# Loading k of the first 512 tokens four tokens to a partition, in a fused attention and feed-forward kernel

## The chip, the cores and the metric

The kernel runs on one core of one Trainium2 chip. The metric is the device time of one execution in microseconds (us). Engines: PE multiplies matrices, DVE (VectorE), ACT (ScalarE) and POOL (GpSimd) work on tiles, SP issues the transfers.

## The reference

Linear attention with a decay per head, on 4 batches x 8 heads x 768 tokens x 64, then a feed-forward layer (FFN) without activation on 3072 rows of 512:

```
for each block of tokens:                       # lam: one decay per head
    intra = ((q k^T) * Dmask) v                 # Dmask[i,j] = lam^(i-j) for i >= j
    inter = (q * lam^(pos+1)) kv_state
    out   = intra + inter
    kv_state = lam^block * kv_state + (k * lam^(block-1-pos))^T v
x = out as 3072 x 512
y = ((x @ w_a) * (x @ w_b)) @ w_out             # 512 -> 1536 -> 512
```

The kernel works in 24 "units" of 128 tokens, six to a batch. The powers of lam are multiplied onto q and k, so that scores only need a triangular mask.

## The kernel before

FFN groups follow each other; attention of later units is placed between their matmuls by a fixed plan. Before the first FFN group the attention of units 0 to 3 must be done. Only that part changes. All loads go through one queue in program order: q, k, v of the first four units, then w_a and w_b in chunks of 512 KB.

```python
q4_r = q[0, :, 0:PACK * BLK, :].rearrange("h (p r) d -> p h (r d)", r=PACK)   # PACK = 4
for i in range(2):                       # q: four tokens to a partition, 1 KB runs, four heads each
    t = wst_pool.tile([128, 1024], F32, name="q4", tag="wst")
    nc.sync.dma_start(out=..., in_=q4_r[:, 4 * i:4 * i + 4])
for w in "kv":                           # k and v: unit by unit, one token to a partition
    for u in range(n0):                  # n0 = 4
        load_x(w, u)                     # [128 tokens, 8 heads, 64], runs of 256 bytes
pump()                                   # then the weights
# ... cut: q scaled and transposed in two halves of four heads ...
for u in range(n0):
    start_unit(u, "pool" if u else "dve")      # scale k: unit 0 on DVE, 1 to 3 on POOL
transpose_k(0); warm(6)                        # warm(n): n idle matmuls
for u in range(n0 - 1):
    transpose_k(u + 1)
    piece_S(u)                                 # scores on PE, two masks on DVE
    warm(4)
make_vb(0, "pool"); kv_update(0); kv_copy(0, "act")
kq3 = scores(3)
make_vb(1, "pool")
for u in range(n0):
    if 0 < u < n0 - 1:
        kv_update(u)                           # state matmuls, all in one PSUM bank
        kv_copy(u, "act" if u < 2 else "dve")  # state to SBUF
        make_vb(u + 1, "pool")
    inter(u)                                   # q with the state: needs the copy of unit u-1
    if u == n0 - 1:
        cast_w("a", 0, "dve")
    intra(u)                                   # masked scores with v
    warm(4)
    # ... cut: masks of unit 3 ...
    evac_o(u, xT, col)                         # o_ps to the FFN's input, on ACT
cast_w("b", 0, "dve")
```

Later units scale k on DVE or POOL and q on POOL, and cast v on POOL (units 4 to 6) or DVE (from 7). Banks of PSUM, the memory that PE writes, come from a ring of seven, of which the idle matmuls hold one until the FFN starts.

## Time and profile before

| | before |
|---|---|
| time, median of 3 (lowest to highest) | 237.23 us (237.14 to 237.46) |
| span in the profile | 235.5 us |
| busy: PE / DVE / ACT / POOL | 96% / 48% / 39% / 22% |
| first FFN matmul | 20.33 us |
| last output of units 0 to 3 | 19.40 us |

In a line of the timeline, the first number is the start in us from the span's start, the second the length, then engine, source line, operation, result and operands; the bracket at the end tells how long the engine was idle before and what ended it. In the chain of waits each step is what released the next.

### The profile page before, as it was taken

The page shows a single profiled execution, that of the slowest core. Times are in us where ns is not written, and L with a number is a line of the kernel's source. Part 1 is how long each engine was busy: PE and PEld are TensorE (multiplying, and loading weights), DVE is VectorE, ACT ScalarE, POOL GpSimd, SP SyncE. Part 2 cuts the span into 40 slices and gives each one's busy share as a digit, 9 for nine tenths or more (in the row PEclk, how much of TensorE's full clock was granted, in tenths as well). Part 3 has the DMA queues.
Part 4 walks back from the last instruction along what each step waited for, and adds up shares of the span by engine and source line. Part 5 has one row for each costly group of instructions (what it writes and reads, how often), then busy time and mean ns, then how long its engine had stood idle before and what let it go on. Part 6 is the DMA issues. An engine that isn't in the chain of part 4 may idle for free.

```text
span 235.5 us, 4537 instructions
## 1 busy us (share of the span) xinstructions
PE 226.3 (96%) x1767; PEld 125.6 (53%) x1767; DVE 113.2 (48%) x200; ACT 91.6 (39%) x172; POOL 51.1 (22%) x64
## 2 busy tenths in 40 slices
PE   7597999999999999999999999999999999999994
PEld 2464444458698754454544454544454544444494
DVE  0584756835558637665135575035565215332050
ACT  3463665046455542342143242142341242332151
POOL 6360000144344743303305503003300000000000
PEclk9999999999999999999999999999999999999999
DMA  4999999999999999999929959713120210000311
GB/s 153 234 245 351 348 357 346 281 214 274 238 236 211 216 171 235 253 190 150 224 91 215 186 60 219 170 62 85 36 47 0 89 71 23 0 0 0 121 60 49
DMA packets 97382, 38.32 MB, mean 163 GB/s; under 512 B 85328, under 2 KB 92880, under 8 KB 97360
## 3 DMA queue, kind: packets, MB, share of 16 engines
q1 hardware_dynamic: 97216, 38.02, 73.1%
q8 instruction: 14, 0.23, 0.5%
q14 instruction: 8, 0.07, 0.1%
q10 hardware_dynamic: 144, 0.00, 0.0%
HBM read 28.32 MB, written 6.29 MB: 147 GB/s over the span
## 4 chain that ended last, share of the span: by engine, by line
PE 88%; SPq 5%; DMA 3%; ACT 1%; DVE 1%; issue 1%; DVEq 0%
PE a_ps L401 27%; PE b_ps L401 27%; PE op L422 26%; SPq L125 5%; DMA wst<-in_moe_w_a_dram 3%; PE o_ps L338 2%; PE kq L314 2%; PE kvd L357 2%; PE o_ps L330 1%; PE tps L291 1%; ACT o_sb L417 1%; SPq L202 0%; DVE wa_sb L158 0%; DVE m L322 0%; ACT xT L345 0%
## 5 line engine op out<-in xcount | busy, mean ns | idle before, releaser
L413 DVE TENSOR_TENSOR ab<-a_sb,b_ps 128x512 bf16<-128x512 bf16 (+2 forms) x96 | 52.6, 552 | 80.9 <-PE b_ps L401 58.8
L401 PE MATMUL a_ps<-xT,wa_sb 128*128 128x512 bf16 (+2 forms) x384 | 77.1, 326 | 1.8 <-DVE wa_sb L158 1.2
L401 PE MATMUL b_ps<-xT,wb_sb 128*128 128x512 bf16 (+2 forms) x384 | 77.2, 326 | 0.0
L408 ACT CAST a_sb<-a_ps 128x512 bf16<-128x512 f32 (+2 forms) x96 | 45.6, 481 | 65.1 <-PE a_ps L401 64.2
L422 PE MATMUL op<-wo_sb,ab 128*128 128x512 bf16 (+2 forms) x312 | 65.6, 363 | 0.0
L401 PEld LDWEIGHTS <-wb_sb 128*128 128x128 bf16 x384 | 34.5, 98 | 28.6
L401 PEld LDWEIGHTS <-wa_sb 128*128 128x128 bf16 x384 | 33.6, 98 | 28.7 <-DVE wa_sb L158 1.4
L422 PEld LDWEIGHTS <-ab 128*128 128x128 bf16 x312 | 28.6, 98 | 30.2
L322 DVE TENSOR_TENSOR m<-kq,lotri 128x512 bf16<-128x512 f32 x48 | 29.9, 682 | 21.3 <-PE kq L314 21.2
L253 POOL TENSOR_TENSOR qk<-kf,lp_k 128x512 bf16<-128x512 f32 x20 | 21.5, 1073 | 81.7 <-issue 31.4
L417 ACT COPY o_sb<-op 128x512 f32<-128x512 f32 (+2 forms) x26 | 14.2, 554 | 37.2 <-PE op L422 37.2
L258 POOL TENSOR_TENSOR qk<-qf,lp_q 128x512 bf16<-128x512 f32 x20 | 22.2, 1111 | 26.3 <-DMA qf<-in_q_dram 26.3
L345 ACT CAST xT<-o_ps 128x512 bf16<-128x512 f32 x24 | 13.2, 589 | 17.4 <-PE o_ps L338 17.3
L370 DVE TENSOR_TENSOR st<-kvd,bdiag 128x512 bf16<-128x512 f32 x18 | 12.3, 684 | 4.4 <-PE kvd L357 4.4
L293 ACT COPY qkT<-tps 128x1024 bf16<-128x1024 bf16 x7 | 7.1, 1012 | 10.9 <-PE tps L291 10.9
L191 PE MATMUL idle<-idle_sb 128*128 128x128 bf16 (+1 forms) x55 | 8.6, 292 | 1.3 <-DVE idle_sb L186 1.3
L338 PE MATMUL o_ps<-m,vb 128*64 128x128 bf16 x192 | 8.2, 223 | 0.0
L267 DVE CAST vb<-vf 128x512 bf16<-128x512 f32 x17 | 7.9, 466 | 0.0
L357 PE MATMUL kvd<-vb,qk 128*128 128x128 bf16 x80 | 7.8, 219 | 0.0
L357 PEld LDWEIGHTS <-qk 128*128 128x128 bf16 x80 | 5.9, 98 | 3.4 <-ACT st L368 0.2
L330 PEld LDWEIGHTS <-st 128*128 128x128 bf16 x80 | 5.5, 98 | 2.8 <-DVE st L370 0.2
L314 PEld LDWEIGHTS <-qkT 64*128 64x128 bf16 x192 | 5.4, 94 | 2.4 <-issue 0.6
(42 smaller groups left out, 74.4 us busy)
## 6 DMA issues: line engine op xcount, KB each, us to landing
kf<-in_k_dram SPq DMA_DIRECT2D x24, 256.0 KB, 5.0
vf<-in_v_dram SPq DMA_DIRECT2D x24, 256.0 KB, 5.0
out_dram<-o_sb SPq DMA_DIRECT2D x23, 256.0 KB, 2.2
qf<-in_q_dram SPq DMA_DIRECT2D x20, 256.0 KB, 4.4
wst<-in_moe_w_a_dram SPq DMA_DIRECT2D x6, 512.0 KB, 8.6
wst<-in_moe_w_b_dram SPq DMA_DIRECT2D x6, 512.0 KB, 8.7
wst<-in_moe_w_out_dram SPq DMA_DIRECT2D x6, 512.0 KB, 8.5
q<-in_q_dram SPq DMA_DIRECT2D x2, 512.0 KB, 5.5
```

Of the source, the lines that this page charges most:

```text
L253: eng_of(eng).tensor_mul(qk[:, 1], raw.pop((u, "k")), lp_k[:, u % NB].to_broadcast([128, H, D]))
L258: eng_of(eng).tensor_mul(U[u]["qk"][:, 0], raw.pop((u, "q")), lp_q[:, u % NB].to_broadcast([128, H, D]))
L322: nc.vector.tensor_mul(m, kq[i], lotri_bc)
L338: nc.tensor.matmul(d["o"][p, hp, :], lhsT=d["vb"][:, 2 * hp + i, :], rhs=d["m"][i][:, hp, :], start=(u % NB == 0 and hp == 0), stop=True, ...
L345: nc.scalar.copy(xT[:, :, col:col + BLK], o_ps)
L357: nc.tensor.matmul(kv["ps"][:, hp, :, :], lhsT=d["qk"][:, 1, 2 * hp:2 * hp + 2, :], rhs=d["vb"][:, 2 * hp:2 * hp + 2, :], start=(nb == 0 a ...
L370: nc.vector.tensor_mul(st[:].rearrange("p hp i d -> p hp (i d)"), kv["ps"][:].rearrange("p hp i d -> p hp (i d)"), bdiag_bc)
L401: nc.tensor.matmul(ps[:, :gt], lhsT=w_sb[:, s, f * 128:(f + 1) * 128], rhs=xT[:, s, :gt], start=(s == 0), stop=(s == KS - 1))
L408: nc.scalar.copy(a_sb[:, :gt], ps[:, :gt])
L413: nc.vector.tensor_mul(ab[:, f, :gt], a_sb[:, :gt], ps[:, :gt])
L417: nc.scalar.copy(o_sb[:, lo:hi], op[:, lo:hi])
L422: nc.tensor.matmul(op[:, lo:hi], lhsT=ab[:, f, t * 128:(t + 1) * 128], rhs=wo_sb[:, f, lo:hi], start=(f == 0), stop=(f == FC - 1))
```

## The change

The intent: k of the first 512 tokens goes through the queue as fast as q, in 1 KB runs, so that w_a comes sooner. Its transposed form comes out as q's does. The natural form (tokens on partitions), which the state needs, is then made by transposing back. The states after units 0, 1 and 2 are summed in three banks at once, so that no state matmul waits for the copy before it.

```diff
-    for w in "kv":
-        for u in range(n0):
-            load_x(w, u)
+    for w, src in (("q", q), ("k", k)):
+        x4_r = src[0, :, 0:PACK * BLK, :].rearrange("h (p r) d -> p h (r d)", r=PACK)
+        for i in range(2):
+            ...
+    for u in range(n0):
+        load_x("v", u)
 # ... cut
+    def scale4(w, i):                    # half i: four heads
+        for eng, rs in ((nc.vector, slice(0, 3)), (nc.gpsimd, slice(3, 4))):
+            eng.tensor_mul(...)          # three quarters on DVE, one on POOL
+    def natural_k(i, eng):
+        tps = ps_bank("tn", [128, PACK, 2, 128], BF16)
+        # 8 transposes of kT back, one copy of 128x1024
 # ... cut
+    for i in range(2):
+        scale4("q", i); transpose4("q", i); warm(4)
+    for i in range(2):
+        scale4("k", i); transpose4("k", i); warm(4)
     for u in range(n0):
+        make_vb(u, "pool")
+    scores4(0)                           # four heads of all four units; 4 banks, then 4 masks
+    natural_k(0, "act")
+    warm(4)
+    scores4(1)
+    natural_k(1, "act")
+    sts = [ps_bank("kv0", ...), ps_bank("kv1", ...), kv_bank()]
+    for hh in range(2):
+        for u, ps in enumerate(sts):
+            for w in range(u + 1):
+                kv_mms(ps, w, range(2 * hh, 2 * hh + 2), w == 0)
+            if hh:
+                kv_copy(u, ps, ("act", "dve", "act")[u])
     for u in range(n0):
         inter(u)
         intra(u)
-        warm(4)
+        warm(2)
+        evac_o(u, *xTs[u], eng="dve" if u == 2 else "act")
+    cast_w("a", 0, "both")               # half on DVE, half on POOL
```

More of the change, by code (lines that the diff above doesn't have):

```diff
@@ L156, in cast_w @@
             nc.scalar.copy(dst, t)
+        elif eng == "both":
+            nc.vector.tensor_copy(dst[:, :, :128], t[:, :, :128])
+            nc.gpsimd.tensor_copy(dst[:, :, 128:], t[:, :, 128:])
         else:
@@ L196 @@
                                                 ap=[[0, 128], lam.ap[0]]))
-    q4 = []
-    q4_r = q[0, :, 0:PACK * BLK, :].rearrange("h (p r) d -> p h (r d)", r=PACK)
-    for i in range(2):
-        t = wst_pool.tile([128, 1024], F32, name="q4", tag="wst")
-        nc.sync.dma_start(out=t[:].rearrange("p (h x) -> p h x", h=4),
-                          in_=q4_r[:, 4 * i:4 * i + 4])
-        q4.append(t[:].rearrange("p (h r d) -> p h r d", h=4, r=PACK))
-        staged["q4", i] = t
-    for w in "kv":
-        for u in range(n0):
-            load_x(w, u)
+    x4 = {}
+    for w, src in (("q", q), ("k", k)):
+        x4_r = src[0, :, 0:PACK * BLK, :].rearrange("h (p r) d -> p h (r d)", r=PACK)
+        for i in range(2):
+            t = wst_pool.tile([128, 1024], F32, name=w + "4", tag="wst")
+            nc.sync.dma_start(out=t[:].rearrange("p (h x) -> p h x", h=4),
+                              in_=x4_r[:, 4 * i:4 * i + 4])
+            x4[w, i] = t[:].rearrange("p (h r d) -> p r h d", h=4, r=PACK)
+            staged[w + "4", i] = t
+    for u in range(n0):
+        load_x("v", u)
     pump()
@@ L235 @@
     lp_q = singles.tile([128, NT, H, 1], F32, name="lp_q")
-    lp_k = singles.tile([128, NB, H, 1], F32, name="lp_k")
+    lp_k = singles.tile([128, NT, H, 1], F32, name="lp_k")
     nc.vector.tensor_mul(tmpe, _bc(loglam, [loglam.ap[0], [0, NT], loglam.ap[1]]),
@@ L239 @@
     nc.scalar.activation(lp_q[:, :, :, 0], tmpe, AF.Exp)
-    nc.scalar.activation(lp_k[:, :, :, 0], tmpe[:, :NB], AF.Exp, scale=-1.0)
+    nc.scalar.activation(lp_k[:, :, :, 0], tmpe, AF.Exp, scale=-1.0)
     lotri_bc = _bc(lotri, [lotri.ap[0], [0, HP], lotri.ap[1]])
@@ L254, in make_ks @@
                                lp_k[:, u % NB].to_broadcast([128, H, D]))
-        U[u] = dict(qk=qk)
+        U[u] = dict(qk=qk, kn=qk[:, 1])
     def make_qs(u, eng):
@@ L294, in piece_T @@
         d["qT"], d["kT"] = qkT[:, 0], qkT[:, 1]
-    def transpose_k(u):
-        d = U[u]
-        tps = ps_bank("tpk", [128, HP, 128], BF16)
-        for hp in range(HP):
-            nc.tensor.transpose(tps[:, hp, :], d["qk"][:, 1, 2 * hp:2 * hp + 2, :], ident)
-        qkT = qkT_pool.tile([128, 2, HP, 128], BF16, name="qkT", tag="qkT")
-        nc.scalar.copy(qkT[:, 1], tps)
-        d["kT"] = qkT[:, 1]
     def score_banks():
@@ L318, in masks, with mask @@
     def masks(u, kq):
-        U[u]["m"] = []
+        ms = mask(kq)
+        U[u]["m"] = lambda i, hp: ms[i][:, hp, :]
+    def mask(kq):
+        ms = []
         for i in range(2):
@@ L322, in masks @@
             nc.vector.tensor_mul(m, kq[i], lotri_bc)
-            U[u]["m"].append(m)
+            ms.append(m)
+        return ms
     def inter(u):
@@ L338, in intra @@
                 nc.tensor.matmul(d["o"][p, hp, :], lhsT=d["vb"][:, 2 * hp + i, :],
-                                 rhs=d["m"][i][:, hp, :], start=(u % NB == 0 and hp == 0),
+                                 rhs=d["m"](i, hp), start=(u % NB == 0 and hp == 0),
                                  stop=True, skip_group_check=True)
@@ L347, in evac_o, with kv_mms, kv_bank, kv_copy @@
             nc.vector.tensor_copy(xT[:, :, col:col + BLK], o_ps)
-    def kv_update(u):
-        d = U[u]
-        nb = u % NB
-        if nb == NB - 1:
-            return
-        if nb == 0:
-            kv["ps"] = kvps_pool.tile([128, HP, 2, D], F32, name="kvd", tag="kvd")
-        for hp in range(HP):
-            nc.tensor.matmul(kv["ps"][:, hp, :, :], lhsT=d["qk"][:, 1, 2 * hp:2 * hp + 2, :],
-                             rhs=d["vb"][:, 2 * hp:2 * hp + 2, :],
-                             start=(nb == 0 and hp == 0), stop=True, skip_group_check=True)
-    def kv_copy(u, eng="dve"):
+    def kv_mms(ps, w, hps, first):
+        d = U[w]
+        for hp in hps:
+            nc.tensor.matmul(ps[:, hp, :, :], lhsT=d["kn"][:, 2 * hp:2 * hp + 2, :],
+                             rhs=d["vb"][:, 2 * hp:2 * hp + 2, :], start=(first and hp == 0),
+                             stop=True, skip_group_check=True)
+    def kv_bank():
+        kv["ps"] = kvps_pool.tile([128, HP, 2, D], F32, name="kvd", tag="kvd")
+        return kv["ps"]
+    def kv_update(u):
         if u % NB == NB - 1:
             return
+        if u % NB == 0:
+            kv_bank()
+        kv_mms(kv["ps"], u, range(HP), u % NB == 0)
+    def kv_copy(u, ps, eng="dve"):
         st = st_bufs[u % 4]
@@ L367, in kv_copy @@
                 p = slice(64 * i, 64 * i + 64)
-                nc.scalar.copy(st[p, :, i, :], kv["ps"][p, :, i, :])
+                nc.scalar.copy(st[p, :, i, :], ps[p, :, i, :])
         else:
             nc.vector.tensor_mul(st[:].rearrange("p hp i d -> p hp (i d)"),
-                                 kv["ps"][:].rearrange("p hp i d -> p hp (i d)"), bdiag_bc)
+                                 ps[:].rearrange("p hp i d -> p hp (i d)"), bdiag_bc)
     def piece_S(u):
@@ L377, in piece_V @@
         kv_update(u)
-        kv_copy(u)
+        if u % NB < NB - 1:
+            kv_copy(u, kv["ps"])
     xTs = {}
@@ L479, with transpose4 @@
     new_xT(0)
-    scratch = ab_pool.tile([128, FC, 512], BF16, name="scratch", tag="ab")
-    qs4 = scratch[:, 0:4, :].rearrange("p r (h d) -> p r h d", d=D)
-    qT4 = scratch[:, 4:8, :]
-    for i in range(2):
-        hs = slice(4 * i, 4 * i + 4)
-        nc.vector.tensor_mul(qs4[:, :, hs, :].rearrange("p r h d -> p h r d"), q4[i],
-                             lp_q[:, NB:, hs, :].rearrange("p r h o -> p h r o")
-                             .to_broadcast([128, 4, PACK, D]))
-        tps = ps_bank("tq", [128, 2, PACK, 128], BF16)
+    scr = [ab_pool.tile([128, FC, 512], BF16, name="scratch", tag="ab") for _ in range(2)]
+    xs4 = {"q": scr[0][:, 0:4, :], "k": scr[1][:, 0:4, :]}
+    xT4 = {"q": scr[0][:, 4:8, :], "k": scr[1][:, 4:8, :]}
+    kn4 = scr[1][:, 8:12, :].rearrange("p u (h d) -> p u h d", d=D)
+    def scale4(w, i):
+        hs = slice(4 * i, 4 * i + 4)
+        dst = xs4[w].rearrange("p r (h d) -> p r h d", d=D)[:, :, hs, :]
+        tab = (lp_q if w == "q" else lp_k)[:, NB:, hs, :]
+        for eng, rs in ((nc.vector, slice(0, 3)), (nc.gpsimd, slice(3, 4))):
+            n = rs.stop - rs.start
+            eng.tensor_mul(dst[:, rs].rearrange("p r h d -> p h r d"),
+                           x4[w, i][:, rs].rearrange("p r h d -> p h r d"),
+                           tab[:, rs].rearrange("p r h o -> p h r o").to_broadcast([128, 4, n, D]))
+        staged.pop((w + "4", i))
+    def transpose4(w, i):
+        tps = ps_bank("t" + w, [128, 2, PACK, 128], BF16)
         for j in range(2):
@@ L491 @@
                 h = 4 * i + 2 * j
-                nc.tensor.transpose(tps[:, j, r, :], qs4[:, r, h:h + 2, :], ident)
-        nc.scalar.copy(qT4[:, 2 * i:2 * i + 2, :].rearrange("c hp (p r) -> c hp p r", r=PACK),
+                nc.tensor.transpose(tps[:, j, r, :], xs4[w][:, r, h * D:(h + 2) * D], ident)
+        nc.scalar.copy(xT4[w][:, 2 * i:2 * i + 2, :].rearrange("c hp (p r) -> c hp p r", r=PACK),
                        tps[:].rearrange("c j r p -> c j p r"))
-        staged.pop(("q4", i))
+    def natural_k(i, eng):
+        tps = ps_bank("tn", [128, PACK, 2, 128], BF16)
+        for u in range(PACK):
+            for j in range(2):
+                nc.tensor.transpose(tps[:, u, j, :],
+                                    xT4["k"][:, 2 * i + j, u * BLK:(u + 1) * BLK], ident)
+        dst = kn4[:, :, 4 * i:4 * i + 4, :].rearrange("p u h d -> p u (h d)")
+        src = tps[:].rearrange("p u j x -> p u (j x)")
+        if eng == "act":
+            nc.scalar.copy(dst, src)
+        else:
+            nc.vector.tensor_copy(dst, src)
@@ new lines, with scores4 @@
+    ms4 = {}
+    def scores4(i):
+        kqs = []
+        for up in range(PACK // 2):
+            kq = score_banks()
+            for uu in range(2):
+                cols = slice((2 * up + uu) * BLK, (2 * up + uu + 1) * BLK)
+                for j in range(2):
+                    for par in range(2):
+                        p = slice(64 * par, 64 * par + 64)
+                        nc.tensor.matmul(kq[par][:, 2 * uu + j, :],
+                                         lhsT=xT4["k"][p, 2 * i + j, cols],
+                                         rhs=xT4["q"][p, 2 * i + j, cols],
+                                         start=True, stop=True, skip_group_check=True)
+            kqs.append(kq)
+        for up, kq in enumerate(kqs):
+            ms4[i, up] = mask(kq)
@@ L496 @@
+    for u in range(n0):
+        U[u] = dict(kn=kn4[:, u], qT=xT4["q"][:, :, u * BLK:(u + 1) * BLK],
+                    m=lambda i, hp, u=u: ms4[hp // 2, u // 2][i][:, 2 * (u % 2) + hp % 2, :])
+    for i in range(2):
+        scale4("q", i)
+        transpose4("q", i)
         warm(4)
-    def start_unit(u, eng):
-        make_ks(u, eng)
-        U[u]["qT"] = qT4[:, :, u * BLK:(u + 1) * BLK]
+    for i in range(2):
+        scale4("k", i)
+        transpose4("k", i)
+        warm(4)
     for u in range(n0):
-        start_unit(u, "pool" if u else "dve")
@@ L504 @@
-    transpose_k(0)
-    warm(6)
-    for u in range(n0 - 1):
-        transpose_k(u + 1)
-        piece_S(u)
-        warm(4)
-    make_vb(0, "pool")
-    kv_update(0)
-    kv_copy(0, "act")
-    kq3 = scores(3)
-    make_vb(1, "pool")
+        make_vb(u, "pool")
+    scores4(0)
+    natural_k(0, "act")
+    warm(4)
+    scores4(1)
+    natural_k(1, "act")
+    sts = [ps_bank("kv0", [128, HP, 2, D], F32), ps_bank("kv1", [128, HP, 2, D], F32), kv_bank()]
+    for hh in range(2):
[4 more added lines that the diff above has]
+                kv_copy(u, ps, ("act", "dve", "act")[u])
@@ L515 @@
     for u in range(n0):
-        if 0 < u < n0 - 1:
-            kv_update(u)
-            kv_copy(u, "act" if u < 2 else "dve")
-            make_vb(u + 1, "pool")
         inter(u)
-        if u == n0 - 1:
-            cast_w("a", 0, "dve")
         intra(u)
-        warm(4)
-        xT, col = xTs[u]
-        if u == 0:
-            masks(3, kq3)
-        evac_o(u, xT, col)
+        warm(2)
+        evac_o(u, *xTs[u], eng="dve" if u == 2 else "act")
+    cast_w("a", 0, "both")
     bank["held"].clear()
```

## The prediction

> **What bounds the kernel now.** The page gives PE 96% busy and a chain that is PE for 88% of the span, so most of the kernel can't be moved by work on the other engines. The diff touches only what runs before the first feed-forward (FFN) group, so I asked two things: when does PE begin its unbroken stretch, and what releases it? The chain of waits between 17 and 24 us answers (start, length, what):
>
> ```profile
> 13.07 6.49 DMA wst<-in_moe_w_a_dram
> 19.58 0.71 DVE wa_sb L158
> 20.33 1.90 PE a_ps L401 x8
> 22.23 0.86 PE b_ps L401 x4
> ```
>
> The reader is to see that the FFN starts at 20.33 us, and that the first chunk of w_a, landed at 19.58, and its cast release it. From there to 41.45 the table of windows has PE busy 21.12 of 21.12 us. So the change is worth what it moves of this 20.33, and hardly more. The runner-up comes from the timeline of 8 to 21 us: the attention of the first four units must also be done, and its last step ends at 18.81 + 0.59 = 19.40, only 0.9 us before.
>
> ```profile
> 8.19 4.83 SPq L125 DMA_DIRECT2D vf<-in_v_dram  x4
> 11.78 4.87 DVE L322 TENSOR_TENSOR m<-kq,lotri 128x512 bf16<-128x512 f32 x8 [2.49 <-PE kq L314]
> ...
> 18.81 0.59 ACT L345 CAST xT<-o_ps 128x512 bf16<-128x512 f32 x1 [0.47 <-PE o_ps L338]
> 19.58 0.69 DVE L158 CAST wa_sb<-wst 128x1024 bf16<-128x1024 f32 x1 [1.61 <-DMA wst<-in_moe_w_a_dram]
> ```
>
> See that the eight masks run back to back: 4.87 us, a pace of 0.609 each. They are the longest piece of vector work here. Why w_a is late shows in the DMA view, first of 4 to 6 us (q in flight), then of 8 to 10 us (k in flight):
>
> ```profile
> DMA packets 789, 0.74 MB, mean 371 GB/s; under 512 B 79, under 2 KB 789, under 8 KB 789
> DMA packets 1731, 0.44 MB, mean 218 GB/s; under 512 B 1731, under 2 KB 1731, under 8 KB 1731
> ```
>
> q, loaded four tokens to a partition, goes in packets of about 1 KB at 371 GB/s; k goes in 256-byte packets at 218 GB/s. w_a waits its turn behind q, k and v in one queue.
>
> **What the Trainium skill says.** (1) "DMA: Bandwidth & Descriptors", Specifications, wants at least 512 B in a transfer for line rate. The trace agrees: 371 against 218 GB/s. (2) "SBUF — State Buffer", Who interferes with whom: a VectorE operation with two SBUF inputs, or in a two-port mode, and a GpSimd one that reads SBUF lock each other out. The trace agrees in this pair (timeline of 42 to 60 us) and in the cast's minimum, median and maximum, where one cast of six took 1533 instead of 692 ns, with the GpSimd multiplication (42.70 to 43.75) in the middle of it:
>
> ```profile
> 42.16 2.13 DVE L158 CAST wo_sb<-wst 128x1024 bf16<-128x1024 f32 x2
> 42.70 1.05 POOL L258 TENSOR_TENSOR qk<-qf,lp_q 128x512 bf16<-128x512 f32 x1 [25.34 <-DMA qf<-in_q_dram]
> ...
> L158 DVE CAST wo_sb<-wst x6: 686/692/1533, 37.8 to 46.3; 128x1024 bf16<-128x1024 f32 x6
> ```
>
> (3) "PSUM — Partial Sum Buffer", Specifications: eight banks. The code holds one for the idle matmuls and one for the state, so six rotate. No wait in this trace is put down to a bank, but the new order uses them harder.
>
> **The change part by part.**
>
> *Transfers.* k's 1 MB needs 1.05 MB / 218 GB/s = 4.8 us now and 1.05 / 360 = 2.9 us as 1 KB pieces: 1.9 us less. v still goes in 256-byte pieces. So w_a lands at 19.58 - 1.9 = about 17.7; half of its cast moves to GpSimd, the rest is 0.35 us on DVE. This bound falls to about 18.1. If nothing else moved, the FFN would start at the attention's 19.40, about 0.9 us sooner.
>
> *k arrives in halves of heads, not by units.* Now unit 0's k is scaled at 8.60 and its scores are masked from 11.78, while k of units 1 to 3 is still landing. In the change every score needs a whole half of the heads. The q halves landed at 5.86 and 7.3, one every 1.45 us, so the k halves land at about 8.75 and 10.2.
>
> *Scaling.* DVE took 1.226 us for a half of q (1024 elements); three quarters is about 0.93. GpSimd takes 1.04 us for 512 elements, so some 0.55 for 256. Side by side 0.93; if they lock each other out, 1.5. *Removed:* one DVE and three GpSimd scalings (0.69 and 3 x 1.04) and four ACT copies of 0.59; *added:* two ACT copies of 1.01 for kT and two for natural k (4.0 us against the 2.4 removed, so ACT has 1.7 more), and 16 transposes on PE (0.06 us each when packed).
>
> *The path to the end, with locking.* k's second half 10.2, scaled 11.75, transposed 12.45 (eight take 0.62), four warm matmuls 12.6. PE is in order and the scores of the first half stand behind these transposes, so they start only now: first bank full at 13.05. Eight masks at 0.609 end at 13.05 + 4.95 = 18.0. (The second half's scores wait for score banks to be freed by masks 2 and 3, at 14.95, still ahead of mask 7 at 16.8.) The DVE copy of state 1 stands behind them in DVE's order: 18.6. Then inter and intra of unit 2, and of unit 3.
>
> ACT: its second natural-k copy needs a bank that mask 4 frees at 15.55, plus transposes: 16.25 to 17.25. The state matmuls of the second half follow; copies of states 0 and 2 (0.74 each) 17.6 to 19.1; then the outputs of units 0, 1 and 3 at 0.59 to 0.6 each: 20.9. Output 2 is on DVE, ending about 20.1. FFN start 20.95, **0.6 us later** than now.
>
> *Without locking* all of it is about 0.6 earlier: 20.35, the same as now.
>
> The three states, in banks of their own, take away the old per-unit wait (state matmul, copy, next state matmul on the same bank; now 0.17 and 0.36 us waits at 15 to 17 us). PE pays 12 more state matmuls (24 for 12), at 0.055 us 0.7 us, in a stretch where it waits anyway.
>
> *After the start.* Weights lead by about 2 us more, but PE already never waits for one in 20.33 to 41.45, so this is worth nothing. The rest should shift rigidly.
>
> **Rivals.** (A) *The w_a wait is the whole story:* then the start moves to 18.5 to 19.4, and the time to about 235.4 to 236.3. For it: the trace names only w_a at the start. Against: the attention is 0.9 us behind, and the change delays the masks' start from 11.78 to some 12.4 to 13.05. (B) *DVE's masks and the ACT tail become the bound*, as summed: 237.2 to 237.9. For it: the masks are the longest piece, they start later and their pace is fixed. (C) *Bank waits and lockouts chain up worse than I sum*, each bank's release costing a round trip between engines: start near 22, time 238.9. For it: kq, tn and state banks all wait on masks. Against: every such wait in my sum ends before DVE needs the result.
>
> **Range and chances.** The two sums of B give a start of 20.35 and 20.95, mean 20.65, or +0.3: 237.23 + 0.3 = 237.5, and I put 237.6, with a little for C. An 8-in-10 range of 236.3 to 238.8 takes in A's slow end and nearly all of C. Faster by 2% would need 4.7 us, and the whole of w_a's wait beyond the attention is 0.9; slower by 2% would need a start at 25. So 0.01, 0.98 and 0.01.
>
> **What would show it.** In the changed profile: k at some 350 GB/s and w_a landing near 17.7 (right if 17.2 to 18.3); first FFN matmul at 20.3 to 21.0, released not by w_a but by the last output on ACT; eight masks beginning at 12.4 to 13.1 and ending by 18.1; GpSimd's quarter-scalings in turn with DVE's, not beside them. I am wrong if masks start before 12 us, if the scores' bank waits leave gaps between masks, if w_a still releases the FFN, or if PE gains or loses over 0.5 us after its start.

## The result, and the profile after

| | before | after |
|---|---|---|
| time, median of 4 | 237.34 us (237.14 to 237.47) | 239.03 us (238.85 to 239.12) |
| span in the profile | 235.5 us | 237.3 us |
| first FFN matmul | 20.33 us | 21.41 us |
| last copy of an output (o_sb) | 232.44 us | 233.99 us |

The ratio is 1.0071, with a 95% interval of 1.0053 to 1.0088. A ratio is the mean time of one kernel's fast runs over that of the other's fast runs of the same rounds, so it is not quite the ratio of the medians. The change made the kernel 1.7 us slower, which is outside the range foretold.

The chain of waits of the changed kernel between 9 and 24 us (start, length, what; "issue" steps and one of idle matmuls are left out between the lines) shows that w_a is gone from it:

```profile
2.39 7.93 DMA k<-in_k_dram
10.40 1.39 POOL scratch L495
11.84 0.45 PE tk L505 x5
12.51 0.38 PE kq L533 x8
12.95 2.49 DVE m L320 x4
15.48 0.62 PE tn L513 x8
16.12 1.02 ACT scratch L518
17.19 0.51 PE kv L351 x6
...
18.38 0.22 PE idle L194 x2
18.60 0.22 PE o_ps L329 x4
18.82 0.34 PE o_ps L337 x8
...
20.78 0.59 ACT xT L344
21.41 0.38 PE a_ps L405
```

The second half of k arrives at 10.33 us. It is scaled and transposed; only behind these transposes, in PE's order, come the scores of the first half; the fourth mask frees a bank at 15.44; natural k of the second half is made in it; then PE is never idle from 17.19 to 20.76 (twelve state matmuls, 0.85 us, and the four units with their idle pairs), and the last output goes to ACT. The lines of the timeline that answer to those of the kernel before:

```profile
12.95 4.87 DVE L320 TENSOR_TENSOR m<-kq,lotri 128x512 bf16<-128x512 f32 x8 [1.64 <-PE kq L533]
16.88 0.61 POOL L159 CAST wa_sb<-wst 128x512 bf16<-128x512 f32 x1 [1.26 <-DMA wst<-in_moe_w_a_dram]
20.60 0.42 DVE L158 CAST wa_sb<-wst 128x512 bf16<-128x512 f32 x1
20.78 0.58 ACT L344 CAST xT<-o_ps 128x512 bf16<-128x512 f32 x1 [0.59 <-PE o_ps L337]
```

w_a has landed at 16.88, 2.7 us earlier than before, and waits 4.5 us to be used. The last output copy, which ended at 19.40 before, ends at 21.37; ACT had been idle for 0.59 us in front of it, waiting for PE.

To see where the rest went, I compared the start of each of the 96 ACT casts of a_ps (the FFN's first product), and of the 26 output copies, with those of the kernel before. The changed kernel is 1.07 us behind through all of groups 0 and 1 and most of group 2, goes from +1.07 to +1.55 between 75.8 and 78.6 us, and stays there to the last copy, +1.55. That is 1.07 us in front of the FFN and 0.48 in group 2; the median times differ by 1.69, and the 0.14 left over I take as variation of the end (four executions of the changed kernel had spans of 237.1 to 237.3). The DVE and POOL timelines of the kernel before at that place:

```profile
72.06 0.42 DVE L267 CAST vb<-vf 128x512 bf16<-128x512 f32 x1
...
72.73 2.47 DVE L322 TENSOR_TENSOR m<-kq,lotri 128x512 bf16<-128x512 f32 x4
...
72.13 1.25 POOL L253 TENSOR_TENSOR qk<-kf,lp_k 128x512 bf16<-128x512 f32 x1 [2.45 <-PE b_ps L401]
```

and of the changed kernel:

```profile
73.14 1.09 DVE L270 CAST vb<-vf 128x512 bf16<-128x512 f32 x1
...
74.48 2.47 DVE L320 TENSOR_TENSOR m<-kq,lotri 128x512 bf16<-128x512 f32 x4
...
72.91 1.04 POOL L261 TENSOR_TENSOR qk<-qf,lp_q 128x512 bf16<-128x512 f32 x1
```

Before, DVE's cast of v came first, by 0.07 us, and POOL's scaling of k took 1.25 instead of 1.04 us, which cost nothing. After, POOL had its k 0.22 us sooner (landed at 71.75, against 71.97) while the cast came 1.08 us later, and so the cast met POOL's next scaling, that of q, already running; it took 1.09 instead of 0.42 us, and the four masks behind it and then PE were late.

### The profile page after: what moved, and what is told of

It reads as the page before. It is cut to its first block, busy times and chain, and to the rows that moved or that the text cites. A ratio compares the mean times of both kernels' runs of the same rounds, so it can differ in the third digit from the quotient of the medians.

```text
span 237.3 us, 4532 instructions
## 1 busy us (share of the span) xinstructions
PE 227.0 (96%) x1758; PEld 126.8 (53%) x1781; DVE 113.5 (48%) x202; ACT 92.5 (39%) x171; POOL 53.6 (23%) x66
## 4 chain that ended last, share of the span: by engine, by line
PE 88%; DMA 5%; ACT 2%; DVE 2%; issue 1%; SPq 1%; POOL 1%; DVEq 0%
PE a_ps L405 26%; PE b_ps L405 26%; PE op L426 26%; DMA k<-in_k_dram 3%; PE o_ps L337 3%; PE kq L308 2%; PE kvd L351 2%; PE o_ps L329 2%; DVE m L320 1%; DMA out_dram<-o_sb 1%; PE tps L294 1%; ACT o_sb L421 1%; SPq L206 1%; POOL scratch L495 1%; ACT xT L344 0%
## 5 line engine op out<-in xcount | busy, mean ns | idle before, releaser
L426 PE MATMUL op<-wo_sb,ab 128*128 128x512 bf16 (+2 forms) x300 | 64.3, 362 | 0.9 <-issue 0.5
L256 POOL TENSOR_TENSOR qk<-kf,lp_k 128x512 bf16<-128x512 f32 x17 | 17.9, 1051 | 80.2 <-issue 31.4
L344 ACT CAST xT<-o_ps 128x512 bf16<-128x512 f32 x23 | 12.5, 589 | 17.0 <-PE o_ps L337 17.0
L373 DVE TENSOR_TENSOR st<-kvd,bdiag 128x512 bf16<-128x512 f32 x17 | 11.6, 682 | 3.8 <-PE kvd L351 3.8
L270 DVE CAST vb<-vf 128x512 bf16<-128x512 f32 x17 | 8.5, 499 | 0.0
L337 PE MATMUL o_ps<-m,vb 128*64 128x128 bf16 x192 | 8.2, 223 | 0.0
L329 PEld LDWEIGHTS <-st 128*128 128x128 bf16 x80 | 5.5, 98 | 2.6
L270 POOL CAST vb<-vf 128x512 bf16<-128x512 f32 x7 | 4.7, 673 | 8.7 <-DMA vf<-in_v_dram 8.7
L337 PEld LDWEIGHTS <-vb 128*64 128x64 bf16 x192 | 5.8, 109 | 1.6
L308 PE MATMUL kq<-qkT 64*128 64x128 bf16 x160 | 6.6, 218 | 0.0
```

The lines of the kernel that those rows point to most:

```text
L256: eng_of(eng).tensor_mul(qk[:, 1], raw.pop((u, "k")), lp_k[:, u % NB].to_broadcast([128, H, D]))
L270: eng_of(eng).tensor_copy(vb, vf)
L337: nc.tensor.matmul(d["o"][p, hp, :], lhsT=d["vb"][:, 2 * hp + i, :], rhs=d["m"](i, hp), start=(u % NB == 0 and hp == 0), stop=True, skip_g ...
L344: nc.scalar.copy(xT[:, :, col:col + BLK], o_ps)
L373: nc.vector.tensor_mul(st[:].rearrange("p hp i d -> p hp (i d)"), ps[:].rearrange("p hp i d -> p hp (i d)"), bdiag_bc)
L426: nc.tensor.matmul(op[:, lo:hi], lhsT=ab[:, f, t * 128:(t + 1) * 128], rhs=wo_sb[:, f, lo:hi], start=(f == 0), stop=(f == FC - 1))
```

## The experiments

The theory after the result has two parts: the FFN starts later because a new chain, through whole halves of k, a bank that waits for a mask, and PE's in-order work, has replaced the wait for w_a; and the half microsecond in group 2 is the lockout of DVE by POOL. **Rivals**: the transfers are worth nothing after all; the stall in group 2 has another cause; the start is set by the masks alone. The kernel before was run in the same rounds; its medians in the four sets were 237.57, 237.89, 237.90 and 237.56, with single executions up to 239.8. These chips vary more than a few tenths of a us, so readings below half a microsecond rest on places in the traces, and the times are beside them. A trace is of one execution of each run. In delay_before, tuned and tuned2 it is one of the fastest of six (238.68, 237.61 and 237.48 us, against medians of 239.41, 238.34 and 237.76), so their places in the table look better than their medians.

All runs but one gave the reference's result. The column "locked" gives the ns that a scaling of k near 58 us, or a cast of v near 73 us (up to 75), took on DVE beyond its usual 685 and 420; "lost" is what PE fell further behind in that group. Starts and last copies are in us against the kernel before.

| run | FFN start | locked at 58, lost in group 1 | locked at 73, lost in group 2 | lost in group 3 | last copy | ratio (95%) |
|---|---|---|---|---|---|---|
| changed kernel | +1.07 | none, 0 | 672, 0.47 | 0 | +1.55 | 1.0071 (1.0053 to 1.0088) |
| k_transfer_only | -1.90 | none, 0 | none, 0 | 0.32 | -1.59 | 0.991 (0.9879 to 0.9941) |
| delay_before | +1.35 | 160, 0.16 | 64, 0 | 0.24 | +1.76 | 1.0064 (1.0038 to 1.009) |
| vb9_act | +1.12 | none, 0 | cast is on ACT, 0 | 0.40 | +1.52 | 1.0055 (1.0028 to 1.0083) |
| nat_first | +0.37 | 473, 0.47 | 783, 0.59 | 0.14 | +1.56 | 1.0043 (1.0019 to 1.0067) |
| no_warm_again | +0.80 | 190, 0.19 | 484, 0.29 | 0 | +1.28 | 1.0036 (1.0006 to 1.0067) |
| dve_scale | +1.04 | 223, 0.22 | 514, 0.32 | 0 | +1.58 | 1.0046 (1.0015 to 1.0077) |
| one_state_bank | +2.75 | none, 0 | 797, 0.60 | 0 | +3.35 | 1.0118 (1.0083 to 1.0153) |
| late_loads | +1.02 | none, 0 | none, 0 | 1.19 | +2.20 | 1.0052 (1.0026 to 1.0078) |
| late_one | +1.03 | 681, 0.68 | 461, 0.27 | 0 | +1.98 | 1.0061 (1.0043 to 1.0078) |
| tuned | +0.03 | none, 0 | none, 0 | 0 | +0.03 | 1.0014 (0.998 to 1.0048) |
| tuned2 | -0.35 | none, 0 | 185, 0 | 0 | -0.35 | 0.9995 (0.9969 to 1.0021) |

At these two places the loss follows the lengthening: in group 1 it is the lengthening itself, in five runs of five; in group 2 it is the lengthening less about 0.2 us of slack, in six of six, with nothing lost where it was 185 or less. Elsewhere it cost nothing: in tuned a scaling of k took 1.29 us (at 51.27) and a cast of v 1.27 (at 67.34), in delay_before a cast of v 1.27 (at 77.97, in group 2 too), and PE fell no further behind there. So a lockout in itself is no loss; these two are places where PE was soon to need what stood behind it on DVE.

Four kernels with starts from +0.37 to +1.12 end within +1.52 to +1.58. Whether something later in the kernel holds them there was not tested; tuned and tuned2, which differ from the changed kernel only in front of the FFN, end at +0.03 and -0.35.

### k_transfer_only: the transfers alone

```diff
 # in the kernel before
-        load_x("k", u)
+        # two heads of 512 tokens in 1 KB runs into the tile of unit u: wrong places, same bytes
+        nc.sync.dma_start(out=t (as 128 x 2 x 256),
+            in_=k[0, 2 * u:2 * u + 2, 0:512, :].rearrange("h (p r) d -> p h (r d)", r=4))
```

> The kernel before, with k of the first four units fetched in 1 KB packets into the same four tiles, so that the values are in the wrong places (wrong results on purpose) and everything else is as before. It prices the transfers alone. If the w_a wait was the bound and the transfers give what was estimated, w_a lands near 17.7 instead of 19.58 us and the FFN starts at 18.4 to 18.6, so 235.3 to 235.9. If the attention of the first units binds right behind (19.40 us now, with k no earlier use to it), the start is 19.4 and the time 236.4.

Measured: 235.3 us (wrong results, on purpose), FFN start 18.44. The end of its chain of waits:

```profile
17.81 0.59 ACT xT L350
18.44 1.67 PE a_ps L406 x7
```

The transfers are worth 1.9 us at the start. w_a is no longer in the chain: it was cast from 16.88, and the last output, which had itself come a microsecond sooner because k did, released the FFN. So the reorganisation around the transfers costs the rest: from -1.90 to +1.07, some 3.0 us.

### delay_before: only later

```diff
 # in the kernel before, ahead of the first FFN matmul
+    warm(11, 512)
+    warm(1)
```

> The kernel before, with idle matmuls put in front of its first FFN matmul so that the FFN starts near 21.4 us (now 20.33), as it does in the changed kernel; nothing else differs. Theory 1 (the half microsecond lost in group 2 of the changed kernel comes only from the FFN running later against the transfers): the time rises by more than the delay, to 238.7 to 239.0, and a VectorE cast of v in group 2 takes over 1 us. Theory 2 (it comes from the loads being issued earlier in the changed kernel): the time rises by the delay alone, 1.05 us, to 238.4, with no such cast.

Measured: 239.41 us. The start went 1.35 us back, 0.3 more than planned. PE lost 0.16 in group 1, where a scaling of k on DVE took 0.84 us, and 0.24 in group 3, but nothing in group 2: the cast near 73 was lengthened by 64 ns only, and the next one, at 77.97, took the 1.27 us that the first theory wanted but cost nothing. So merely running later did not bring the loss in group 2; it brought others. Neither theory's number came out: a delay of 1.35 became 1.76.

### vb9_act: the locked cast moved to ACT

```diff
-        make_vb(u, "pool" if u < n0 + 3 else "dve")
+        make_vb(u, "pool" if u < n0 + 3 else "act" if u == 9 else "dve")
```

> The changed kernel, with one cast alone moved: v of unit 9, in group 2, is cast by ACT instead of VectorE. Theory (that cast is locked out by the GpSimd multiplication at 72.9 us, takes 1.09 instead of 0.42 us, delays four masks and with them PE): the changed kernel's stall of 0.48 us in group 2 goes, FFN start stays at 21.4, time 238.5 to 238.6. Rival (the stall has another cause, such as a PSUM bank or the ACT queue): 239.0 as the changed kernel.

Measured: 239.07 us. The DVE timeline where the changed kernel has its stall:

```profile
73.64 0.42 DVE L417 TENSOR_TENSOR ab<-a_sb,b_ps 128x256 bf16<-128x256 bf16 x1 [0.37 <-ACT a_sb L412]
73.98 2.47 DVE L320 TENSOR_TENSOR m<-kq,lotri 128x512 bf16<-128x512 f32 x4
```

The masks start at 73.98 instead of 74.48, and PE passes group 2 with no loss. The cast itself has gone from DVE too, so this alone would not tell its usual 0.42 us from its lengthening; with the table, where the loss follows the lengthening, the lockout is the cause there. The time did not follow, since 0.40 us was lost in group 3 instead, where the chain goes through a transposing transfer:

```profile
97.55 5.83 DMA qkT<-qk
103.38 0.05 issue
103.42 0.40 PE kq L308 x8
```

Its input had been made by POOL, which had waited for a load of k until 95.28 (94.23 in the changed kernel). Why that load was later is not shown.

### nat_first: the bank wait taken away

```diff
-    scores4(1)
     natural_k(1, "act")
+    scores4(1)
```

> The changed kernel, with the second half's natural form of k made before the second half's scores instead of after them, so that its bank no longer waits for the fourth mask. Theory (the chain to the FFN goes through that bank wait, mask 4 to natural k to the state matmuls): the state matmuls start near 15.9 instead of 17.19, the chain goes over to the eight masks and the VectorE copy of state 1, FFN start 20.5 to 20.7 instead of 21.41, time 238.1 to 238.4. Rival (the masks alone, or PE's own in-order work after 17.2, set the start whatever feeds them): start 21.2 to 21.4, time 238.9.

Measured: start 20.71, at the edge of what was expected; time 238.83, later than the 238.1 to 238.4 expected. The chain of waits from the fourth mask on:

```profile
12.97 2.49 DVE m L320 x4
15.47 0.04 issue
15.51 0.38 PE kq L533 x7
15.89 0.44 PE kv L351 x6
```

All 24 state matmuls now run in one piece from 15.89 to 17.33; in the changed kernel twelve ran in PE's wait from 15.92 and the other twelve from 17.19 to 18.04. The fourth mask still holds PE, now by the bank that the scores need; from there PE's work runs through as before. The 0.70 us won were lost again, 0.47 and 0.59 us, to lockouts in groups 1 and 2.

### no_warm and no_warm_again: PE's own work in the unit loop

```diff
         intra(u)
-        warm(2)
         evac_o(u, *xTs[u], eng="dve" if u == 2 else "act")
```

> The changed kernel without the two idle matmuls per unit in the loop over the first four units. Theory (from 17.2 us on PE's own in-order work sets the FFN start, and these pairs cost 0.22 us each in it, three of them before the last output): FFN start 20.7 to 20.8 instead of 21.41; the time follows less surely, 238.2 to 238.8, for the later stretches may lose or gain half a microsecond by their phase. Rival (state copies on ACT and VectorE set the pace of the units): start 21.2 to 21.4.

In no_warm the profile fell on an execution of 240.06 us in which q and k landed 1.4 us late and the clock was at 0.50 from 10 to 12 us: start 22.63, no use for the question (all six executions: median 239.34, ratio 1.0063).

> The same kernel as no_warm, whose profile fell on an execution in which q and k landed 1.4 us late and the clock was at half for 8 to 12 us. Theory now (most of what an idle pair seems to cost is a gap that PE has anyway between 64-column and 128-column matmuls, so that a pair is worth about 0.1 us): with q and k landing at 5.9 and 10.3 as usual, FFN start 21.1 to 21.2. Theory first put down (0.22 us a pair): 20.7 to 20.8. Rival: without the pairs the clock drops in every execution, start 21.4 or later.

Measured: start 21.14, time 238.71, clock 1.0. In the chain of waits, the same stretch without the idle pairs:

```profile
18.04 0.34 PE o_ps L337 x8
18.38 0.39 PE o_ps L329 x4
18.77 0.34 PE o_ps L337 x8
19.11 0.33 PE o_ps L329 x4
```

Four inter matmuls (L329) take 0.22 us behind an idle pair but 0.33 to 0.39 directly behind the 64-column intra matmuls (L337). So a pair's 0.22 us holds 0.11 of matmuls and 0.11 of a gap that PE has anyway. The Trainium skill's "TensorEngine Tiling (Array Packing)", under Key Properties, says that "Changing tiling mode (not just tile) drains the TensorE"; the trace agrees, with 0.11 us, if that is the reason. Removing three pairs gave 0.27 us, not 0.66.

### dve_scale: is the split of the scaling a loss?

```diff
-        for eng, rs in ((nc.vector, slice(0, 3)), (nc.gpsimd, slice(3, 4))):
+        for eng, rs in ((nc.vector, slice(0, 4)),):
```

> The changed kernel with the four scalings of q and k wholly on VectorE instead of three quarters there and one quarter on GpSimd. Theory (the two engines lock each other out, so the split takes 1.44 us where VectorE alone takes 1.23): k's second half is scaled by 11.6 instead of 11.79, FFN start 21.2. Rival (the GpSimd part is slow by itself and hides beside VectorE): VectorE alone takes 1.23 as well, so the two can be told apart only by the GpSimd durations in the changed kernel's trace; a start of 21.4 or later would say the split was no loss.

Measured: 239.0 us, start 21.38. DVE alone took 1.23 us and was done at 11.59, against 11.79; but PE then did all eight transposes behind it (0.62 us), where in the changed kernel only five were left (0.45 in the chain, the others done while POOL worked). Masks started at 12.91 and 12.95. So POOL's quarter does take turns with DVE (1.39 us for 256 elements, of which DVE's 0.96 comes first), but the split is no loss in the end: the expected gain did not come.

### one_state_bank: one part undone

```diff
-    sts = [ps_bank("kv0", ...), ps_bank("kv1", ...), kv_bank()]
-    for hh in range(2): ...
+    kv_update(0)
+    kv_copy(0, kv["ps"], "act")
     for u in range(n0):
+        if 0 < u < n0 - 1:
+            kv_update(u)
+            kv_copy(u, kv["ps"], "act" if u < 2 else "dve")
         inter(u)
```

> The changed kernel with one part undone: the kv state of the first four units is again accumulated in one bank, unit by unit, with its copy between. Theory (the three banks take away a wait of state copy before next state matmul): the units go at the pace of the kernel before, about 1.2 us each, and the FFN starts at 21.9 to 22.3 instead of 21.41. Rival (the units' own PE work binds, the banks are worth nothing): 21.3 to 21.5.

Measured: 240.81 us, start 23.09, later than the 21.9 to 22.3 expected. The table of windows shows one thing that was not foreseen (columns: stretch and length, then busy us and instructions of PE, weight loads, DVE, ACT, POOL; the granted clock; the DMA engines' share and GB/s):

```profile
14.00:17.00 3.00, 1.49 (x26) 0.98 (x18) 3.00 (x6) 1.54 (x2) 1.26 (x3) 1.00 1.06 322
17.00:20.00 3.00, 2.80 (x29) 1.84 (x30) 0.82 (x2) 2.19 (x6) 0.57 (x1) 0.55 1.09 353
```

PE was busy half of 14 to 17 us (2.08 us in the changed kernel, whose clock stayed at 1.0), and the clock was then at 0.55 for three; that the one brought the other is not shown. The record helps a little: the four executions with a mean clock of 0.993 took 240.59 to 241.27 us, the one with 0.999 took 240.16, still over a microsecond more than the changed kernel's 238.85 to 239.12 in its own set. So the banks seem to be worth something, but how much of the 1.7 us at the start is theirs and how much the clock's stays open.

### late_loads and late_one: the distance between PE and the loads

```diff
+    pending += [("x", 0), ("x", 1)]      # two loads of 512 KB that nothing reads (late_one: one)
     pending += [("o", c) for c in range(4)] ...
```

> The changed kernel with two transfers of 512 KB more, into tiles that nothing reads, behind the last w_a and w_b chunk: they hold back all loads of later units by about 3 us and so restore the distance between PE and the loads that the kernel before has (in the changed kernel the loads come 1.9 us earlier and PE 1.1 us later). Theory (the half microsecond lost in group 2 comes from that distance alone): PE runs 1.07 us behind the kernel before all through with no further loss, last output copy +1.05 to +1.1 instead of +1.55, time 238.3 to 238.6. Rival (the loss has to do with the FFN starting late, or with something else in the changed order): again +1.5 and 238.9 to 239.1.

Measured: 239.24 us. The loss in group 2 was gone, as the theory wanted, but 1.19 us were lost in group 3, where the chain waits on a transposing transfer (5.69 us, to 104.07). So the theory was right on group 2 and wrong on the time.

> As late_loads, with one extra transfer of 512 KB instead of two, so that the loads of later units come about 1.5 us later than in the changed kernel. The two extra transfers took away the loss in group 2 but brought one of 1.06 us in group 3, where a transposing transfer came late. Theory (PE loses in group 2 when the loads run over about 2 us ahead of their place in the kernel before, and in group 3 when they run late; between lies a stretch without loss): with the loads 1.5 us ahead, PE stays 1.0 to 1.1 us behind through group 2, at most 0.25 more is lost in group 3 (as in the kernel before delayed), last copy +1.05 to +1.3. Rival (any disturbance of the loads costs): +1.5 or more.

Measured: 239.01 us; 0.68 us lost in group 1 and 0.27 in group 2, both at DVE instructions that POOL had locked out:

```profile
58.20 1.37 DVE L263 TENSOR_TENSOR qk<-kf,lp_k 128x512 bf16<-128x512 f32 x1
...
57.97 1.04 POOL L268 TENSOR_TENSOR qk<-qf,lp_q 128x512 bf16<-128x512 f32 x1
```

The theory that a certain distance is safe falls. Which of two instructions came first differed by tenths of a microsecond from run to run, and none of the numbers tried here told ahead where a lockout would strike.

### tuned and tuned2: a version of all this

tuned is the changed kernel with natural_k(1) ahead of scores4(1), scaling on DVE alone, all state copies on ACT, outputs 1 and 2 on DVE, no idle pairs in the loop and none ahead of the first scores. tuned2 also moves eight state matmuls into PE's wait for the fourth mask:

```diff
     def scores4(i, between=None):
         for up in range(PACK // 2):
+            if up and between:
+                between()            # states 0 and 2, first half: 2 + 6 matmuls
```

> The changed kernel with what the runs so far point to put together: natural k of the second half before its scores, scaling on VectorE alone, all three state copies on ACT, outputs 1 and 2 on VectorE, no idle matmuls in the unit loop nor before the first scores. Theory (bank wait, lockout and PE's in-order work are what the reorganisation costs): FFN start 19.2 to 19.6, earlier than the 20.33 of the kernel before; time 236.2 to 236.9 where no new collision of VectorE and GpSimd comes up later, up to 237.3 with one. Rival (something else holds the start, such as v's or w_a's landing): start 20.2 or later.

> The run tuned, with eight of the state matmuls moved into PE's wait for the fourth mask. Theory (from the fourth mask on, PE's in-order work sets the start): those 0.44 us leave the chain, FFN start 19.8 to 20.0 instead of 20.37 and 0.4 before the 20.33 of the kernel before; time 236.8 to 237.2 where the kernel before shows 237.3. Rival (the ACT copies of the states set the pace): start 20.2 to 20.4.

Measured: tuned 238.34 us (at most 237.3 expected), start 20.37, later than the 19.2 to 19.6 expected: PE's work from the fourth mask to the last output took 4.5 us (15.25 to 19.72), which I had again summed too low. tuned2: start 20.00, as expected, but 237.76 us, which is 0.14 less than the kernel before in the same set (237.90), where 0.1 to 0.5 less was expected. The chain of waits of tuned2 before the FFN:

```profile
14.76 0.27 PE kv L351 x2
15.04 0.34 PE kvd L351 x6
15.37 0.33 PE kq L535 x8
15.70 0.67 PE kv L351 x10
```

The wait for the mask has left the chain; by the profile it now begins with a load of v, still in 256-byte runs, that lands at 13.96, and its cast on POOL. In its trace tuned2 is 0.35 us ahead of the kernel before all through, and its ratio is 0.9995 (0.9969 to 1.0021): equal to the kernel before within the noise, and better than the changed kernel. No run shows a version that beats both with certainty.

## Why the prediction was wrong

The path was right up to the second natural copy of k; two steps behind it failed: PE's own queue was left out of the last stretch, and the rest did not shift rigidly. By the prediction's own steps:

1. **Transfers**: right for k, too small for w_a. The two halves of k, 0.52 MB each, landed 1.50 and 1.57 us behind the piece before, so at about 350 and 335 GB/s (foretold 360), and k was complete 1.8 us earlier (foretold 1.9). w_a's first chunk had landed by 16.88, 2.7 us earlier and not 1.9, outside the 17.2 to 18.3 allowed; the further 0.9 to 1.0 us lie between the landing of v and that of w_a (2.9 us before, 1.9 after), and no run shows why. It was harmless, as nothing waited for w_a. k_transfer_only shows their worth, 1.9 us.
2. **Rival B, the attention becomes the bound**: right; the FFN is released by the last output, on ACT, and not by w_a. What makes that output late is step 4. Rival A is excluded for the changed kernel. It was the right story for the transfers alone, and there the gain was larger than A's 0.9 to 1.8, since the attention gains from an earlier k too.
3. **Scaling, scores, masks**: right, in its case "with locking". k's second half 10.33 (10.2), scaled 11.79 (11.75), masks 12.95 to 17.82 (13.05 to 18.0), second natural copy 16.12 to 17.14 (16.25 to 17.25), state copies 17.57 to 19.08 (17.6 to 19.1). The price on which it settled was the mean of this case and one without locking; locking came, which is 0.3 us.
4. **ACT's outputs end at 20.9**: failed. The sum put ACT's copies end to end, and said of the added state matmuls that PE pays them "in a stretch where it waits anyway". ACT was idle 0.59 us before the last, since PE had not made it. The term that was missing is PE's own in-order work in the last stretch: 3.57 us from 17.19 to 20.76, with 0.85 for twelve of the state matmuls and 0.22 + 0.34 + 0.22 = 0.78 for each of units 1 to 3 with its idle pair. The start came at 21.41 instead of 20.95: 0.46 us. The runs bear it out: letting that queue begin earlier (nat_first, 0.70 us), taking the idle pairs out of it (no_warm_again, 0.27) and moving eight state matmuls out of it (tuned2 against tuned, 0.37) each moved the start.
5. **"The rest should shift rigidly"**: failed. With a start 1.07 us later and loads that come sooner, POOL came before DVE at one place, and 0.48 us was lost in group 2. vb9_act took that loss away, and in five other runs with a lockout there the loss follows its length. Where it will strike could not be told ahead, so that it cost 0.48 and not nothing is chance.

Together 0.3 + 0.46 + 0.48 make 1.24 of the 1.3 us between the 0.4 us foretold (237.6 against 237.23) and the 1.69 measured.

Rival C, bank waits and lockouts that chain up worse than summed, named a time near the one measured (238.9) with a start near 22. Its bank waits did not come: the one at the fourth mask was in the sum, and ended 0.1 us earlier than there. Its lockouts did in part, one in the scaling (0.3 us against the mean) and one in group 2, but they do not add up to a start near 22; that its time came out so near is partly luck. (The prediction's "No wait in this trace is put down to a bank" does not fit its own 0.17 us wait of a state matmul for the copy of the state's bank; nothing in its sum rests on that.)

## What to carry to other kernels

A faster transfer is worth what it saves only if the consumer can still begin on the first piece; here 1.9 us of transfer were won and 3.0 us given back by an order that waits for whole halves, transposes back and ends in one engine's in-order work (only some of these parts were priced one by one). When pricing a new order, sum each engine's queue through to the end, PE's too, and not only the waits between engines. And in a tightly planned kernel do not count on the rest shifting rigidly: here shifts of at most a few microseconds brought further losses between 0 and 1.2 us, at casts and scalings that DVE and POOL do side by side and at transposing transfers. Look there before explaining a small difference by the change itself.

## What the Trainium skill lacked or had wrong

- "SBUF — State Buffer", Who interferes with whom: confirmed, not lacking, with its rule that the order of issue decides who blocks. In the runs of the table a DVE cast of 0.42 us took up to 1.22 near 73 us (one_state_bank) and a two-input scaling of 0.68 up to 1.37 near 58 us (late_one) while POOL multiplied. What it lacks is what this costs a plan: at those two places the loss on PE was the lengthening itself (group 1) or the lengthening less 0.2 us (group 2), and at others, up to 0.85 us long, nothing.
- "TensorEngine Tiling (Array Packing)", Key Properties: names the drain on a change of mode without its size. Here matmuls of 128 columns behind matmuls of 64 columns came about 0.11 us later.
- "TensorE: Matmul & The Clock Gate", What's actually happening: gives the fall to half clock as coming after an idle window of about 3.4 us. In one_state_bank the clock was at 0.55 from 17 to 20 us although PE had been busy 1.49 us of the three before, with a longest gap of 0.99 us (to 17.20). Another section of the page tells of such falls from short idle times, without saying how much idle it takes.
- "DMA: Bandwidth & Descriptors", Specifications: says that transfers under 512 B miss line rate. Another section of the page gives an overhead for each small packet, but none has a measured rate for such loads from the SP queue. Here 256-byte packets gave 218 GB/s and 1 KB packets 341 to 371.
